# One tile and one transfer per MB of weights, a transfer limit in the planner, and split first transposes

## The chip, the cores and the metric

The kernel runs on one core of one Trainium2 chip. Its time is device microseconds of that core, from launch to end; a profile's span runs from the core's first to its last instruction. Engines are named as in the profile: PE (TensorE, matmul), PEld (its weight loads), DVE (VectorE), ACT (ScalarE), POOL (GpSimd) and SP (SyncE, which here issues nearly all DMAs).

## What is computed

x is 2048 rows of 1024 (bf16). Two layers, each of two steps with the same weights:

```python
x = x + A(layernorm(x), wqkv, wo)
x = x + B(layernorm(x), w1, b1, w2, b2)
...
def A(x, wqkv, wo):          # 32 heads of 32; a window of 8 keys, every second row back
    q, k, v = split(x @ wqkv)
    logits = q . k[pos - 2 * w] / sqrt(32), w = 0..7, masked where pos - 2 * w < 0
    return (softmax(logits) . v) @ wo
def B(x, w1, b1, w2, b2):    # 1024 -> 3584 -> 1024
    return relu(x @ w1 + b1) ** 2 @ w2 + b2
```

## The kernel before, in words

**Units.** Even and odd rows are held apart, so that the window's stride of two becomes one. The 2048 rows of a layer are cut into four blocks of 512; a block of a layer is a unit, u = 0 to 7. A unit goes through SA (load x, layer norm, transpose to `xnA`), the projections to q, k and v (`SQ` plain, `SQ7` with seven products), S2 (attention, mostly DVE), SW or SW7 (projection with wo, layer norm into `xnB`), SF1 (w1, squared relu, into `r2`) and SF2 (w2). `build` interleaves them: while unit u is in SW and SF1, unit u + 1 is in its projections and attention.

**Seven products.** From unit 1 on (SF1), and from unit 2 on (q, k, v), a matrix product of 2 x 2 blocks is made of seven products in place of eight. A step has seven of them, numbered 1 to 7. Products 1, 2 and 4 use raw blocks of the weights; 5, 6, 7 and 3 use combinations (sums and differences of raw blocks), which DVE forms once while the first units run (`keep_wqkv`, `keep_w1`) and which are stored to scratch in DRAM (`wqs`, `w1s`) as 128 x 1024 f16 cells of 256 KB. On the moving side stand the activations `xnA` or `xnB` and their combinations `TA` or `T`. A product is eight matmuls of 256 columns (`product`, L658). `interleave` sets the order: product pr of step i sorts by 7 i + AT[pr], so neighbouring steps overlap. SF1 has seven steps (49 products), the job "k" two (14), the job "qv" four (28).

**Loads of the weights.** `seven` (L564) walks this order in groups of four products. A group has one tile `w` of 128 x 4 x 4 x 256 (1 MB): its raw blocks first, each by a transfer of its own of 256 KB (rows of 2 KB out of the weight matrix), then its combinations, one transfer of 256, 512 or 768 KB from that group's scratch. `cells` says which place in which tile a product has. A product waits for its own place alone.

**The planner.** Nothing is issued as it is written: `Plan.add` collects operations with engine, estimated duration, priority and the cells that they read and write. `Plan.schedule` runs them through a list scheduler with classes of buffers: twelve of 8 KB per partition, of which at most eight for weight tiles `w` (`caps`); the others hold `xnA`, `xnB`, `T`, `TA`, attention products and so on. A DMA is charged `mb / DMA_MBS` on one common line plus a latency. `emit` makes the order that each engine's instructions then have, in order, on the chip; `ORDER` is a list of seeds by which priorities are shifted slightly ahead of each pass. The planner knew no limit to the number of transfers under way. On the chip, SP's transfers use eight semaphores in turn, and SP waits where the one whose turn it is still belongs to a transfer that hasn't landed.

**The start.** In unit 0 the first tiles of x are normalised by DVE (`ln_first`), transposed by PE into PSUM (`transpose`, L802, eight blocks of 128 x 128) and copied by one DVE instruction of 1024 columns into `xnA` (L805). `SQ(0, "kq")` runs its first sixteen chunks for the first half of the rows alone (`halves`); a chunk is eight matmuls (L877) over the eight blocks. Weights of unit 0 come in pieces of 512 KB.

Names of the profile: `in_B_w_dram` at L658 is w1, `in_A_wqkv_dram` wqkv, `w1s`, `wqk` and `wqqv` are scratch of combinations; L402 is the helper `dma`, L768 the transposing DMA.

Of the kernel before, what the change touches and what calls it, by code (L numbers as in the profile page):

```python
# [52 lines left out]
RAW = {1: (0, 0), 2: (0, 1), 4: (1, 1)}  # L53
PR1 = 20.0
# [19 lines left out]
DMA_MBS = 0.38  # L74
OWN_LAT = {"DVE": 0.12, "ACT": 0.1}
# [4 lines left out]
def act(n):  # L80
    return 0.05 + n * 0.00084

# [34 lines left out]
class Plan:  # L117
# [45 lines left out]
    def schedule(self):  # L163
# [46 lines left out]
        dma_free = 0.0  # L210
        out = []
        t = 0.0
        left = len(self.ops)
        while left:
            progress = False
            for e in engs:
# [28 lines left out]
            while True:  # L245
                if own is None:
                    offer((o.prio, next(seq), o))
                elif o is not None:
# [9 lines left out]
                    if not own:  # L258
                        for b in o.bufs:
# [55 lines left out]
class _Kernel:  # L315
# [19 lines left out]
    def setup(self):  # L335
# [36 lines left out]
        self.order1 = self.interleave(range(self.NDP))  # L372
        self.orderq = {"k": self.interleave([("k", 0), ("k", 1)]), "qv": self.interleave([("q", 0), ("q", 1), ("v", 0), ("v", 1)])}
        self.wqs = {j: self.scratch(tc, o, f"wq{j}") for j, o in self.orderq.items()}
        self.two = [tc.dram_tile([128, 2, 4, BLK], F16, name=f"two{i}") for i in range(2)]
        self.w1s = self.scratch(tc, self.order1, "w1s")

# [32 lines left out]
    def wqkv_block(self, nm, ms, n=1):  # L410
        i = 4 * "qkv".index(nm) + ms
        return self.wqkv[i * 128:(i + n) * 128]

    def wqkv_raw(self, d, m, k):
        nm, s = d
        return self.wqkv_block(nm, 2 * m + s)[:, k * 1024:(k + 1) * 1024]

    def w1_raw(self, dp, m, k):
        return self.w1[dp * 128:(dp + 1) * 128, m * 2048 + k * 1024:m * 2048 + (k + 1) * 1024]
# [5 lines left out]
    def cells(self, order):  # L425

        at = {}
        for j in range(0, len(order), 4):
            part = order[j:j + 4]
            raw = [d for d in part if d[1] in RAW]  # L430
            for i, d in enumerate(raw + [d for d in part if d[1] not in RAW]):
                at[d] = j // 4, i, len(raw)
        return at

    def scratch(self, tc, order, name):

        n = [0] * (-(-len(order) // 4))
        for (d, pr), (t, i, r) in self.cells(order).items():
            n[t] += pr not in RAW
        return [tc.dram_tile([128, max(c, 1), 4, 256], F16, name=f"{name}{t}") for t, c in enumerate(n)]  # L440
# [71 lines left out]
    def interleave(self, todo):  # L512

        return [(d, pr) for _, d, pr in sorted((7 * i + AT[pr], d, pr) for i, d in enumerate(todo) for pr in AT)]

    def keep_wqkv(self, nm, ws, after=()):
# [3 lines left out]
        at = self.cells(self.orderq[job])  # L520

        def one(s):
# [5 lines left out]
            def comb(t, a, b, op, r, pr):  # L528
                p.add("DVE", dve(1024), lambda: nc.vector.tensor_tensor(t[:], a(), b(), op), r, [(t, 0)], self.nxt(), after, name="tq")
                j, i, n = at[(nm, s), pr]  # L530
                self.dma(lambda: self.wqs[job][j][:, i - n], lambda: t[:], [(t, 0)], [(("wqs", job, j), i)], 0.26, prio=50.0, name="wqst", lat=4.0)
# [8 lines left out]
    def SQ7(self, u, job):  # L540
# [8 lines left out]
        self.seven(self.orderq[job], self.wqs[job], ("wqs", job), self.wqkv_raw, st["xnA"], st["TA"], lambda d: self.qkv_step(u, *d))  # L549
# [14 lines left out]
    def seven(self, order, store, key, raw, xnT, T, make):  # L564

        rhs = self.rhs_blocks(xnT, T)
        at = self.cells(order)
        self.ffs = []
        steps, ws = {}, {}
        for d, pr in order:  # L570
# [12 lines left out]
            if d not in steps:  # L583
                steps[d] = make(d)
            steps[d](pr, ws[t], i, *rhs[pr])
# [7 lines left out]
    def qkv_step(self, u, nm, s):  # L593
# [29 lines left out]
        def mul(pr, w, wi, rhs, rc):  # L623
            bank, fm = self.product(pr, w, wi, rhs, X, Y, Z)
            self.state[u]["gate" + nm] = p.add("PE", 8 * MMH, fm, rc + [(w, wi)], [(bank, 0)], self.nxt(), name="fq")
# [36 lines left out]
    def keep_w1(self, dp, w):  # L662

        nc, p = self.nc, self.p
        at = self.cells(self.order1)
# [4 lines left out]
        def store(pr, src, r):  # L670
            j, i, n = at[dp, pr]
            self.dma(lambda: self.w1s[j][:, i - n], src, r, [(("w1s", j), i)], 0.26, prio=50.0, name="w1st", lat=4.0)
# [41 lines left out]
    def ln(self, x, xv, xcells, xnT, tl, prio, vec, on_pe=False, tag="xn", after=(), vnorm=True):  # L714
# [25 lines left out]
        else:  # L740
# [18 lines left out]
            if vnorm:  # L759
                p.add("DVE", 0.45, f3v, xr + [(sm, 1)], [(xn, 0)], -99.5, name="ln3")  # L760
            else:
                p.add("ACT", 1.15, f3, xr + [(sm, 1)], [(xn, 0)], prio - 0.2, name="ln3")
        if on_pe:
            self.transpose(xn, xnT, tl, -10.0)
            return
# [5 lines left out]
    def ln_first(self, x, xv, xnT, tl, after=()):  # L771
# [19 lines left out]
        def rest(after=()):  # L791
            p.add("DVE", 0.5, f4, [(x, 0), (sm, 0), (sm, 1)], [(xn, 0)], -2e5 + pr, after=after, name="bn4")
            return self.transpose(xn, xnT, tl, -1e5 + pr, act=tl in CP), xn
        return bn, ag, rs, rest

    def transpose(self, xn, xnT, tl, prio, act=False):
        nc, p, KD = self.nc, self.p, self.KD
        pt = Buf("ps", "pt", [128, KD, 128], F16, "partial")

        def f5():  # L800
            for kd in range(KD):
                nc.tensor.transpose(pt[:, kd, :], xn[:, kd * 128:(kd + 1) * 128], self.ident[:])  # L802

        def f6():
            (nc.scalar.copy if act else nc.vector.tensor_copy)(xnT[:, tl], pt[:])  # L805
        p.add("PE", 0.65, f5, [(xn, 0)], [(pt, 0)], prio, name="pt")
        return p.add("ACT" if act else "DVE", 1.05 if act else 0.69, f6, [(pt, 0)], [(xnT, tl)], prio - 200.0, name="ptc")
# [11 lines left out]
    def SA(self, u):  # L819
        layer, b = divmod(u, self.NB)  # L820
# [26 lines left out]
    def SQ(self, u, jobs, order=None, halves=()):  # L847
# [10 lines left out]
        for ms in range(4) if u == 0 else (0, 2):  # L858
            for nm in jobs:
                w = ws[nm][ms // 2]  # L860
                if u == 0:
# [8 lines left out]
        def chunk(nm, c0, hs):  # L870
# [4 lines left out]
            def fm():  # L875
                for kd in range(KD):
                    nc.tensor.matmul(pq[:, t0 * HB:t1 * HB], w[:, c0 // 2 % 2, kd // 4, kd % 4, c0 % 2 * 128:c0 % 2 * 128 + 128],  # L877
                                     xnT[:, 2 * t0:2 * t1, kd, :], start=(kd == 0), stop=(kd == KD - 1))
            st["gate" + nm] = self.pe(4 * len(hs), fm, [(xnT, i) for i in range(2 * t0, 2 * t1)] + [(w, c0 // 2 % 2)], [(pq, h) for h in hs], name="pq")
# [3 lines left out]
        for nm, c0 in halves:  # L883
            chunk(nm, c0, (0,))
# [307 lines left out]
    def SF1_plain(self, u):  # L1192
# [8 lines left out]
        def load(dp):  # L1201
            w = Buf("8K", "w", [128, 2, 8, 256], BF)
            for m in range(2):
                self.dma(lambda m=m: w[:, m].rearrange("p k n -> p (k n)"), lambda m=m: self.w1[dp * 128:(dp + 1) * 128, m * 2048:(m + 1) * 2048],
# [38 lines left out]
        for i, (dp, pr) in enumerate(self.interleave(range(PLAIN1, self.NDP))):  # L1243
# [12 lines left out]
    def SF1(self, u):  # L1256
# [8 lines left out]
        self.seven(self.order1, self.w1s, ("w1s",), self.w1_raw, xnT, T, lambda d: self.ffn1_step(r2, d, u in FOLD))  # L1265
        st["gatef"] = self.ffs[40]

    def ffn1_step(self, r2, dp, fold):
# [51 lines left out]
        def mul(pr, w, wi, rhs, rc):  # L1320
            bank, fm = self.product(pr, w, wi, rhs, X, Y, Z)
            self.ffs.append(p.add("PE", 8 * MMH, fm, rc + [(w, wi[0] if isinstance(wi, tuple) else wi or 0)], [(bank, 0)], self.nxt(), name="ff"))
# [218 lines left out]
def _lay(name, a):  # L1541

    if name == "A_wqkv":
# [32 lines left out]
```

## Time and profile before

| | before |
|---|---|
| median of 3 runs, us | 1143.18 (1141.79 to 1144.17) |
| profiled execution, us | 1140.7 |
| its span, us | 1139.0 |
| mean granted clock of PE | 0.998 |
| DMA packets | 176799, 362.37 MB |
| HBM read, written | 314.84 MB, 31.46 MB |

How to read it: a row of a group gives busy time, the mean of one instruction in ns, and the idle time just ahead of it with what ended it. A wait row reads "engine line of who waited <- engine, tile and line of what it waited for: total us, times, longest". SPq is SP's queue, that is, its issuing of DMAs. In a row of stretches stand, after the stretch and its length, each engine's busy us with its number of instructions, the granted clock, the DMA engines' share, and GB/s. A matmul's busy time includes its passage through the array, so neighbours overlap; a product of eight matmuls advances PE by less than its busy time. The DMA share of a stretch can be over 100%.

### The profile page before, as it was taken

How to read it: one execution, taken by the hardware profiler on the slowest of the kernel's cores; microseconds unless marked ns; L12 is line 12 of the kernel's file. 1: busy time of each engine (PE TensorE's matmuls, PEld its weight loads, DVE VectorE, ACT ScalarE, POOL GpSimd, SP SyncE). 2: the span in 40 equal slices, each digit the busy share in tenths (PEclk: the TensorE clock that was granted, in tenths of full speed). 3: DMA queues.
4: the chain of work that ended last, by engine and by line, in shares of the span. 5: the costliest groups of instructions: out<-in, count | busy, mean ns of one | idle time of the engine just before them, and what ended most of it. 6: DMA issues, size and time to landing. Idle time of an engine off the chain costs nothing.

```text
span 1139.0 us, 20967 instructions
## 1 busy us (share of the span) xinstructions
PE 1124.7 (99%) x7873; PEld 772.6 (68%) x7919; DVE 998.5 (88%) x1539; ACT 802.2 (70%) x1602; POOL 1.8 (0%) x8
## 2 busy tenths in 40 slices
PE   8999999998999999999999999999999999999998
PEld 6645764677846787468864688657885678845864
DVE  7999999998699998979999699996999889996341
ACT  6734997567984789757994679847798477943861
POOL 0000000000000000000000000000000000000000
PEclk9999999999999999999999999999999999999999
DMA  9967679999999998999979997899989999699982
GB/s 366 290 212 255 223 265 312 326 357 332 399 322 360 331 368 299 333 383 301 397 256 349 403 306 304 314 313 393 318 330 325 377 349 352 256 343 279 368 281 80
DMA packets 176799, 362.37 MB, mean 318 GB/s; under 512 B 71866, under 2 KB 80186, under 8 KB 174778
## 3 DMA queue, kind: packets, MB, share of 16 engines
q1 hardware_dynamic: 176410, 360.51, 93.2%
q8 instruction: 62, 1.02, 0.4%
q10 hardware_dynamic: 288, 0.52, 0.1%
q14 instruction: 39, 0.32, 0.1%
HBM read 314.84 MB, written 31.46 MB: 304 GB/s over the span
## 4 chain that ended last, share of the span: by engine, by line
PE 89%; DVE 4%; ACT 3%; DMA 3%; issue 1%; SPq 0%; DVEq 0%; ACTq 0%
PE X L658 24%; PE X L1375 14%; PE Z L658 12%; PE pq L877 7%; PE Z L1375 7%; PE Y L658 6%; PE py L478 4%; PE py L1071 4%; PE Y L1375 3%; PE X L1142 3%; PE lg L952 2%; PE Z L1142 1%; DMA w<-in_B_w_dram 1%; ACT r L1310 1%; PE Y L1142 1%
## 5 line engine op out<-in xcount | busy, mean ns | idle before, releaser
L658 PEld LDWEIGHTS <-w 128*128 128x128 bf16 (+1 forms) x4904 | 480.0, 98 | 75.6 <-DMA w<-in_B_w_dram 3.6
L1375 PEld LDWEIGHTS <-r 128*128 128x128 f16 x1183 | 115.7, 98 | 135.9 <-issue 1.7
L1375 PE MATMUL X<-w,r 128*128 128x512 f16 (+2 forms) x784 | 176.5, 377 | 1.1 <-ACT yxa L1044 0.5
L937 DVE TENSOR_TENSOR P<-q,k 128x2048 f16<-128x2048 f16 x128 | 154.0, 1224 | 5.0 <-PE lg L952 4.4
L658 PE MATMUL X<-T,w 128*128 128x256 f16 x1224 | 154.7, 274 | 3.3 <-DMA w<-in_B_w_dram 3.3
L1016 DVE TENSOR_TENSOR pr<-pb,v 128x4096 f16<-128x4096 f16 x64 | 146.3, 2296 | 1.1 <-PE X L658 0.7
L945 DVE TENSOR_TENSOR P<-P,P 128x2048 f16<-128x2048 f16 x106 | 129.3, 1221 | 0.3
L1310 ACT ACTIVATE r<-rr 128x1024 f16<-128x1024 f16 x110 | 124.6, 1143 | 1.3 <-DVE rr L1306 1.1
L1023 DVE TENSOR_TENSOR pr<-pr 128x2048 f16<-128x2048 f16 (+1 forms) x128 | 118.4, 953 | 0.1
L658 PE MATMUL X<-TA,w 128*128 128x256 f16 x864 | 108.5, 273 | 0.0
L591 ACT COPY Y<-X 128x512 f32<-128x512 f32 x115 | 69.9, 608 | 27.1 <-PE X L658 22.9
L877 PE MATMUL pq<-xnA,w 128*128 128x256 f16 (+1 forms) x512 | 86.6, 326 | 0.4 <-DMA w<-in_A_wqkv_dram 0.4
L1293 DVE TENSOR_TENSOR rr<-u,y 128x512 f16<-128x512 f16 x110 | 46.3, 423 | 33.2 <-ACT y L1289 17.2
L1289 ACT CAST y<-Z 128x512 f16<-128x512 f32 x110 | 69.3, 647 | 5.3 <-PE Z L658 4.0
L877 PEld LDWEIGHTS <-w 128*128 128x128 bf16 x512 | 49.8, 98 | 33.0 <-DMA w<-in_A_wqkv_dram 0.7
L1316 ACT ACTIVATE rr<-X,b1T 128x256 f16<-128x256 f32 x110 | 55.0, 558 | 5.3 <-PE X L658 5.1
L1316 ACT ACTIVATE rr<-Y,b1T 128x256 f16<-128x256 f32 x110 | 53.3, 531 | 4.3 <-PE Y L658 3.8
L658 PE MATMUL Y<-xnB,w 128*128 128x256 f16 x440 | 56.0, 273 | 0.1
L658 PE MATMUL X<-xnB,w 128*128 128x256 f16 x440 | 55.7, 273 | 0.0
L609 ACT CAST u<-X 128x512 f16<-128x512 f32 x72 | 41.8, 586 | 18.9 <-PE X L658 18.9
L613 ACT CAST yq<-Z 128x512 f16<-128x512 f32 x72 | 41.7, 587 | 18.3 <-PE Z L658 16.5
L658 PE MATMUL Z<-T,w 128*128 128x256 f16 x392 | 50.6, 273 | 0.6 <-DVE halo L913 0.5
(159 smaller groups left out, 1649.9 us busy)
## 6 DMA issues: line engine op xcount, KB each, us to landing
w<-tw SPq DMA_DIRECT2D x56, 896.0 KB, 6.1
w<-in_B_w_dram SPq DMA_DIRECT2D x147, 256.0 KB, 7.5
w<-in_B_w_dram SPq DMA_DIRECT2D x42, 896.0 KB, 7.6
w<-w1s SPq DMA_DIRECT2D x56, 512.0 KB, 7.9
w<-in_A_wqkv_dram SPq DMA_DIRECT2D x108, 256.0 KB, 6.2
w<-w1s SPq DMA_DIRECT2D x28, 768.0 KB, 8.1
w<-wqqv SPq DMA_DIRECT2D x30, 512.0 KB, 6.2
w<-in_B_w_dram SPq DMA_DIRECT2D x28, 512.0 KB, 6.1
```

Source lines behind the costliest of these rows:

```text
L591: self.p.add("ACT", act(512), lambda: self.nc.scalar.copy(Y[:], X[:]), [(X, 0)], [(Y, 0)], UP, name="u")
L658: nc.tensor.matmul(bank[:, a, :], lw[:, k, a * 128:(a + 1) * 128], rhs(k), start=(start and k == 0 and a == 0), stop=(k == 3), skip_group_ ...
L877: nc.tensor.matmul(pq[:, t0 * HB:t1 * HB], w[:, c0 // 2 % 2, kd // 4, kd % 4, c0 % 2 * 128:c0 % 2 * 128 + 128], xnT[:, 2 * t0:2 * t1, kd, ...
L937: nc.vector.tensor_tensor(cur[:], q[:, c, None, hb * HB:(hb + 1) * HB].to_broadcast([128, W, HB]), _win_ap(k[:, c, :], HALO + hb * HB, HB) ...
L945: nc.vector.tensor_tensor(other[:], other[:], cur[:], ALU.add)
L1016: p.add("DVE", dve(4096), lambda pr=pr, ch=ch: nc.vector.tensor_tensor(pr[:], pb[:].unsqueeze(1).to_broadcast([128, 2, W, HB]), _win_ap2(v ...
L1023: nc.vector.tensor_tensor(dst, pr[:, :, 0:n, :], pr[:, :, n:2 * n, :], ALU.add)
L1142: nc.tensor.matmul(bank[q][:], left(j, q), right(j), start=start and j == 0, stop=j == h - 1, skip_group_check=True)
L1289: p.add("ACT", act(512), lambda: nc.scalar.copy(y[:], bank[:]), [(bank, 0)], [(y, 0)], 1.5, name="y")
L1310: p.add("ACT", 0.955, lambda: nc.scalar.activation(out=r2[:, f:f + 2, :].rearrange("p a t -> p (a t)"), in_=r[:].rearrange("p a m t -> p ( ...
L1316: p.add("ACT", 0.36, lambda a=a: nc.scalar.activation(out=r[:, a, 0, :], in_=bank[:, a, :], func=ACTF.Relu, bias=self.b1T[:, f + a:f + a + ...
L1375: nc.tensor.matmul(banks[q][:, lo:hi], left(jj, q), w[:, j, lo:hi], start=(start and jj == 0), stop=(jj == h - 1), skip_group_check=True)
```

## The change

1. **Raw tiles.** All raw blocks are laid out once more in the order of use behind the weight matrix (a rearrangement of the input array), four to a tile: `raw_tiles`. One contiguous transfer of 1 MB with 8 KB rows (256, 512 KB where fewer are left) loads four.
2. **Combination tiles.** The four combinations of a step have one scratch tensor and one tile, loaded by one transfer of 1 MB. `cells` and its places go.
3. **Waits.** A product waits for its whole tile (cell `(w, 0)`).
4. **The planner** refuses a DMA while the seventh-last is still under way in its model (`LANES = 7`), looks at every engine again when a DMA ends, and has new seeds (`ORDER`: 48, 29 and 30 in place of 47, 26 and 18).
5. **First transposes.** For the first two tiles of unit 0, transposes and copies go by halves (four blocks, 512 columns); the first chunk of `SQ(0, "kq")` is two operations of four matmuls, the first of which needs the first halves only.
6. v of unit 0 is loaded in two transfers of 1 MB in place of four of 512 KB.

```diff
+COMB = (5, 7, 6, 3)
+RT = 4
+LANES = 7
...
         def fits(o):
+            if o.mb and len(landed) >= LANES and landed[-LANES] > t + 1e-9:
+                return False
...
                     end = dma_free
+                    landed.append(end + o.lat)
...
                     if not own:
+                        if o.mb:
+                            fresh.update(engs)
...
+    def raw_tiles(self, ap, at, n):
+        tiles = []
+        for i in range(0, n, RT):
+            k = min(RT, n - i) * 1024
+            tiles.append(ap[at:at + 128 * k].rearrange("(p n) -> p n", n=k))
+            at += 128 * k
+        return tiles
...
+    def scratch(self, tc, todo, name):
+        return {d: tc.dram_tile([128, 4, 4, 256], F16, name=f"{name}{i}") for i, d in enumerate(todo)}
...
         for d, pr in order:
-            t, i, nr = at[d, pr]
-            if t not in ws:
-                w = ws[t] = Buf("8K", "w", [128, 4, 4, 256], F16)
-                mine = [(j, e) for e, (s, j, _) in at.items() if s == t]
-                for j, (e, q) in mine:
-                    if q in RAW:
-                        self.dma(lambda w=w, j=j: w[:, j].rearrange("p k n -> p (k n)"), lambda e=e, q=q: raw(e, *RAW[q]), (), [(w, j)], 0.256,
-                                 name="w", cast=BF)
-                cs = [j for j, (e, q) in mine if q not in RAW]
-                if cs:
-                    self.dma(lambda w=w, a=nr, b=nr + len(cs): w[:, a:b], lambda t=t: store[t][:], [(key + (t,), j) for j in cs],
-                             [(w, j) for j in cs], len(cs) * 0.256, name="w")
+            if pr in RAW:
+                if nr % RT == 0:
+                    w = ws["raw"] = Buf("8K", "w", [128, 4, 4, 256], F16)
+                    n = min(RT, 3 * len(self.scr[job]) - nr)
+                    self.dma(lambda w=w, n=n: w[:, 0:n].rearrange("p i k n -> p (i k n)"), lambda t=nr // RT: raws[t], (), [(w, 0)], n * 0.256,
+                             name="w", cast=BF)
+                w, i = ws["raw"], nr % RT
+                nr += 1
+            else:
+                if d not in ws:
+                    w = ws[d] = Buf("8K", "w", [128, 4, 4, 256], F16)
+                    key = (job,) + (d if isinstance(d, tuple) else (d,))
+                    self.dma(lambda w=w: w[:], lambda d=d: self.scr[job][d][:], [(key, i) for i in range(4)], [(w, 0)], 4 * 0.256, name="w")
+                w, i = ws[d], COMB.index(pr)
...
-        p.add("PE", 0.65, f5, [(xn, 0)], [(pt, 0)], prio, name="pt")
-        return p.add("ACT" if act else "DVE", 1.05 if act else 0.69, f6, [(pt, 0)], [(xnT, tl)], prio - 200.0, name="ptc")
+            p.add("PE", 0.65 / parts, f5, [(xn, 0)], [(pt, i)], prio, name="pt")
+            op = p.add("DVE", 0.09 + 0.6 / parts, f6, [(pt, i)], [(xnT, tl if i == parts - 1 else (tl, i))], prio - 200.0, name="ptc")
+        return op
...
+            for i in range(parts):
+                xc = [(xnT, t if i == parts - 1 else (t, i)) for t in range(2 * t0, 2 * t1)]
+                st["gate" + nm] = self.pe(4 * len(hs) / parts, lambda i=i: fm(i), xc + [(w, c0 // 2 % 2)], [(pq, h) for h in hs], name="pq")
...
         for nm, c0 in halves:
-            chunk(nm, c0, (0,))
+            chunk(nm, c0, (0,), 2 if (nm, c0) == halves[0] else 1)
```

More of the change, by code (lines that the diff above doesn't have):

```diff
@@ L81, in act, with interleave @@
     return 0.05 + n * 0.00084
+def interleave(todo):
+    return [(d, pr) for _, d, pr in sorted((7 * i + AT[pr], d, pr) for i, d in enumerate(todo) for pr in AT)]
 def mix(x):
@@ L210, in schedule @@
         dma_free = 0.0
+        landed = []
         out = []
@@ L371, in setup @@
         self.NDP = KF // 4
-        self.order1 = self.interleave(range(self.NDP))
-        self.orderq = {"k": self.interleave([("k", 0), ("k", 1)]), "qv": self.interleave([("q", 0), ("q", 1), ("v", 0), ("v", 1)])}
-        self.wqs = {j: self.scratch(tc, o, f"wq{j}") for j, o in self.orderq.items()}
+        todo = {"k": [("k", 0), ("k", 1)], "qv": [("q", 0), ("q", 1), ("v", 0), ("v", 1)], "w1": list(range(self.NDP))}
+        self.orders = {j: interleave(d) for j, d in todo.items()}
+        self.scr = {j: self.scratch(tc, d, f"s{j}") for j, d in todo.items()}
+        self.raws = {"k": self.raw_tiles(self.wqkv, 3 * D * D, 6), "qv": self.raw_tiles(self.wqkv, 3 * D * D + 6 * 128 * 1024, 12),
+                     "w1": self.raw_tiles(self.w1, D * self.F, 3 * self.NDP)}
         self.two = [tc.dram_tile([128, 2, 4, BLK], F16, name=f"two{i}") for i in range(2)]
-        self.w1s = self.scratch(tc, self.order1, "w1s")
         p = self.p
@@ L423, in w2_block @@
         return self.w2[i * 128:(i + 1) * 128]
[L425 to L440, printed above, removed]
+    def scratch(self, tc, todo, name):
+        return {d: tc.dram_tile([128, 4, 4, 256], F16, name=f"{name}{i}") for i, d in enumerate(todo)}
     def keep_w2(self, j0, n, w):
@@ L548, in SQ7 @@
             st["TA"] = self.rhs_combos(st["xnA"], 1.0, "8K", "TA", True)
-        self.seven(self.orderq[job], self.wqs[job], ("wqs", job), self.wqkv_raw, st["xnA"], st["TA"], lambda d: self.qkv_step(u, *d))
+        self.seven(job, st["xnA"], st["TA"], lambda d: self.qkv_step(u, *d))
         for nm in job:
@@ L759, in ln @@
             if vnorm:
-                p.add("DVE", 0.45, f3v, xr + [(sm, 1)], [(xn, 0)], -99.5, name="ln3")
+                p.add("DVE", 0.45, f3v, xr + [(sm, 1)], [(xn, 0)], pv, name="ln3")
             else:
@@ L763, in ln @@
         if on_pe:
-            self.transpose(xn, xnT, tl, -10.0)
-            return
+            return self.transpose(xn, xnT, tl, -10.0 if pv == -99.5 else pv, parts), xn
         def f5():
@@ L857, in SQ @@
             ws[nm] = [Buf("8K", "w", [128, 2, 2, 4, 256], BF) for _ in range(2)]
-        for ms in range(4) if u == 0 else (0, 2):
+        pieces = u == 0 and len(jobs) > 1
+        for ms in range(4) if pieces else (0, 2):
             for nm in jobs:
                 w = ws[nm][ms // 2]
-                if u == 0:
+                if pieces:
                     self.dma(lambda w=w, ms=ms: w[:, ms % 2].rearrange("p a k n -> p (a k n)"), lambda nm=nm, ms=ms: self.wqkv_block(nm, ms), (),
@@ L868, in SQ, with chunk @@
             order = [(nm, c0) for nm in jobs for c0 in range(NCH)]
-        def chunk(nm, c0, hs):
+        def chunk(nm, c0, hs, parts=1):
             pq = Buf("ps", "pq", [128, BLK], F32)
@@ L1242, in SF1_plain @@
         self.ffs, steps = st["phs"], {}
-        for i, (dp, pr) in enumerate(self.interleave(range(PLAIN1, self.NDP))):
+        for i, (dp, pr) in enumerate(interleave(range(PLAIN1, self.NDP))):
             if dp not in steps:
@@ L1264, in SF1 @@
         T = self.rhs_combos(xnT, -60.0, "8K", "T")
-        self.seven(self.order1, self.w1s, ("w1s",), self.w1_raw, xnT, T, lambda d: self.ffn1_step(r2, d, u in FOLD))
+        self.seven("w1", xnT, T, lambda d: self.ffn1_step(r2, d, u in FOLD))
         st["gatef"] = self.ffs[40]
@@ L1321, in mul @@
             bank, fm = self.product(pr, w, wi, rhs, X, Y, Z)
-            self.ffs.append(p.add("PE", 8 * MMH, fm, rc + [(w, wi[0] if isinstance(wi, tuple) else wi or 0)], [(bank, 0)], self.nxt(), name="ff"))
+            self.ffs.append(p.add("PE", 8 * MMH, fm, rc + [(w, wi[0] if isinstance(wi, tuple) else 0)], [(bank, 0)], self.nxt(), name="ff"))
             if pr == 1:
@@ L1541, in _lay, with raws @@
 def _lay(name, a):
+    import numpy as np
+    def raws(blocks, todo):
+        seq = [blocks(d, *RAW[pr]) for d, pr in interleave(todo) if pr in RAW]
+        return [np.stack(seq[i:i + RT], 1).reshape(-1) for i in range(0, len(seq), RT)]
     if name == "A_wqkv":
-        a = a.reshape(2, 4, 128, 3, 128, 4, 2).transpose(3, 5, 2, 0, 1, 6, 4).reshape(1536, 2048)
+        a = a.reshape(2, 4, 128, 3, 128, 4, 2).transpose(3, 5, 2, 0, 1, 6, 4).reshape(3, 4, 128, 2, 1024)
+        get = lambda d, m, k: a["qkv".index(d[0]), 2 * m + d[1], :, k]
+        a = np.concatenate([a.reshape(-1)] + raws(get, [("k", 0), ("k", 1)]) + raws(get, [("q", 0), ("q", 1), ("v", 0), ("v", 1)]))
     elif name == "A_wo":
```

58 lines of the change are left out of this document (27 added, 31 removed), and 16 rows, old and new, of the table ORDER.

## The prediction

> **What bounds the kernel now.** First the page: busy time of each engine and the DMA queue's share.
>
> ```profile
> span 1139.0 us, 20967 instructions
> PE 1124.7 (99%) x7873; PEld 772.6 (68%) x7919; DVE 998.5 (88%) x1539; ACT 802.2 (70%) x1602; POOL 1.8 (0%) x8
> ...
> q1 hardware_dynamic: 176410, 360.51, 93.2%
> ```
>
> PE is busy for 1124.7 of 1139.0 us, so all its idle time together is 14.3 us. The change alters no product, so no more than that can come back, and part of it lies before the first and after the last matmul. SP's queue holds the 16 DMA engines for 93% of the span: two resources are nearly full. Next, what PE waited for, longest first:
>
> ```profile
> PE X L658 <- DMA w<-in_B_w_dram: 3.3, 1, 3.3
> PE pt L802 <- DVE xn L784: 1.8, 1, 1.8
> ...
> PE X L1375 <- ACT yxa L1044: 0.5, 1, 0.5
> PE Z L658 <- DVE halo L913: 0.5, 1, 0.5
> ```
>
> One wait in the middle is worth looking at: 3.3 us for a raw block of w1. The other long one (1.8 us) is the first layer norm. Around the 3.3 us, the stretches (PE, PEld, DVE, ACT and POOL busy, granted clock, DMA share, GB/s):
>
> ```profile
> 260.00:271.50 11.50, 11.50 (x106) 10.09 (x104) 11.50 (x22) 8.86 (x17) 0.00 (x0) 1.00 1.05 316
> 271.50:274.90 3.40, 0.06 (x2) 0.03 (x2) 3.40 (x6) 0.83 (x2) 0.00 (x0) 0.92 1.01 375
> 274.90:278.40 3.50, 3.50 (x18) 2.31 (x19) 2.20 (x2) 1.60 (x4) 0.00 (x0) 0.59 1.00 351
> 278.40:312.00 33.60, 33.60 (x304) 29.54 (x303) 22.18 (x37) 33.51 (x71) 0.00 (x0) 1.00 1.01 391
> ```
>
> PE stands still for 3.34 us (3.40 less 0.06), and in the 3.5 us behind it the granted clock is 0.59, which costs 3.5 x 0.41 = 1.4 us more. The stop is worth 4.8 us. It falls in SF1 of unit 1. The chain of waits says how it came about:
>
> ```profile
> 255.81 0.87 PE Y L658 x8
> ...
> 257.50 7.28 DMA w<-w1s
> 264.78 0.02 issue
> 264.80 10.03 DMA w<-in_B_w_dram
> ```
>
> The late load was issued 0.02 us after another load had landed and took 10.03 us itself: SP was held by a transfer in flight, not by a buffer. Over the span, SP's own waits:
>
> ```profile
> SPq L402 <- PE X L658: 91.6, 49, 10.9
> SPq L402 <- PE Z L658: 64.6, 18, 10.9
> SPq L402 <- DMA w<-w1s: 57.5, 54, 3.2
> ...
> SPq L402 <- DMA w<-in_B_w_dram: 31.6, 78, 2.3
> ```
>
> It waits longest for PE to give buffers back (156.2 us in two rows), which is harmless, as such loads are ahead of their use; and 89.1 us in two rows, 132 times, for transfers in flight.
>
> **Part 1, fewer and larger loads.** The loads of the seven-product jobs:
>
> ```profile
> w<-in_B_w_dram SPq DMA_DIRECT2D x147, 256.0 KB, 7.5
> ...
> w<-w1s SPq DMA_DIRECT2D x56, 512.0 KB, 7.9
> w<-in_A_wqkv_dram SPq DMA_DIRECT2D x108, 256.0 KB, 6.2
> w<-w1s SPq DMA_DIRECT2D x28, 768.0 KB, 8.1
> ...
> w<-in_A_wqkv_dram SPq DMA_DIRECT2D x6, 1024.0 KB, 9.2
> ```
>
> Before: 147 + 84 for w1, 108 raw ones for q, k, v, and by the code 6 x 4 and 6 x 7 from scratch, 405 in all. After: SF1 takes 6 raw and 7 combined tiles in each of 7 units (91), k 2 + 2 and qv 3 + 4 in each of 6 (66), 157 in all. Bytes are the same; 248 issues leave SP. A 1024 KB load lands in 9.2 us, a 256 KB one in 6.2 to 7.5, so seven in flight hold four times a raw block's bytes. What the engines gain I take from two 4 us stretches, 137.5 to 141.5 us with 2 KB rows nearly alone and 494 to 498 us with 8 KB rows:
>
> ```profile
> DMA packets 864, 1.61 MB, mean 401 GB/s; under 512 B 80, under 2 KB 80, under 8 KB 864
> q1 hardware_dynamic: 864, 1.61, 105.3%
> ```
>
> ```profile
> DMA packets 224, 1.70 MB, mean 426 GB/s; under 512 B 16, under 2 KB 16, under 8 KB 16
> q1 hardware_dynamic: 224, 1.70, 101.6%
> ```
>
> Divided by their shares these are 1.61/4/1.053 = 0.382 and 1.70/4/1.016 = 0.418 MB per us. The 255 raw blocks are 66.8 MB: 174.9 us of the queue's time now, 159.8 after, so 15 us fewer, from 93.2% to about 92% of the span. All of it lies beside PE. It is worth time only where a load is late, which is the one place above; the 10 or so raw blocks just ahead of it (2.6 MB) save 6.9 - 6.3 = 0.6 us there.
>
> **Part 2, what the larger tile costs.** (a) A product now waits for its whole tile, and product 1 of a job needs a raw and a combined tile, 2.1 MB where 1.05 MB did. Counting the interleaved order through, the bytes needed by a given product are equal or 1.05 MB more, never 2; at the tenth product of SF1, where the stop is, they are equal. (b) A tile is held longer: its four products lay next to each other, 4 x 0.87 = 3.5 us; now they spread over 7 to 9 places, up to 7.9 us. SF1 uses 13 tiles in 49 x 0.87 = 42.6 us, one in 3.3. With eight tiles allowed, issue to last use is 8 x 3.3 = 26 us, so 22.7 us to the first use before and 18.3 after; less 8.1 and 9.2 to land, a margin of about 14.6 shrinks to 9. That costs nothing in a steady stretch: SP's long waits for PE are the cover. It begins to cost when only five tiles can be had (16.5 - 7.9 - 9.2 is below zero), because the twelve 8 KB buffers are shared with activations and attention. (c) Stores into scratch stay 256 KB each and as many: nothing. (d) v of unit 0 in two 1 MB loads in place of four: its first use comes long after, nothing.
>
> **Part 3, the planner.** It now refuses a transfer while seven are under way, so SP's order fits what SP really does; and its seeds give another order on every engine. PE's work is the same, so the effect is only in stops. No row prices a new order. Bounds: it takes away the 4.8 us and both stops of 0.5 (-5.8), or leaves them and adds as much (+5.8). I take the long stop gone, because its last link is exactly what the planner now knows and the load behind it is now in one of a third as many transfers; and I add 1.0 us of new short stops, as many as the two rows of 0.5, since an order never fits everywhere.
>
> **Part 4, the first transposes by halves.**
>
> ```profile
> 8.68 1.43 DVE L805 COPY xnA<-pt 128x1024 f16<-128x1024 f16 x2
> ...
> 10.16 1.03 PE L877 MATMUL pq<-xnA,w 128*128 128x256 f16 x8
> 11.61 0.61 PE L877 MATMUL pq<-xnA,w 128*128 128x256 f16 x4 [0.41 <-DMA w<-in_A_wqkv_dram]
> ```
>
> The two copies end at 10.11 and PE starts 0.05 later. In halves, each between 0.36 (half) and 0.71 us (the same), PE's first half can start up to 0.36 earlier. But the next chunk waits for its weights until 11.61, which the change doesn't move, so the gain lies between 0 and 0.7 (0.36 and the wait filled by another chunk). I take 0.3. The two extra copies cost DVE between nothing and 1.4 us; PE's wait for weights until 11.61 covers that, and without it the 1.4 would eat the gain.
>
> **The sum.** -4.8 + 1.0 - 0.3 = -4.1 us. The profiled execution took 1140.7 us (span 1139.0 and 1.7 around it): 1136.6 for one like it. The median of the runs is 2.5 above it, so 1143.2 - 4.1 = **1139.1 us**.
>
> **Rivals.** *The stop stays.* DMA is at 1.05 in 260 to 271.5 and moves only 316 GB/s, against 391 at 1.01 later, so the load may be late for bytes, not for its place in line; freeing SP then changes nothing. For it: the share. Against: 0.6 us less work ahead, another order. Time: 1143.2 - 0.3 = 1142.9.
>
> *Slower: the first tiles of SF1 in unit 1.* The place has no margin:
>
> ```profile
> 252.08 0.33 SPq L402 DMA_DIRECT2D w<-w1s  x1
> ...
> 260.01 1.04 PE L658 MATMUL X<-xnB,w 128*128 128x256 f16 x8
> ```
>
> ```profile
> w<-w1s SPq DMA_DIRECT2D x1, 512.0 KB, 7.9
> ```
>
> The first combined part lands at 260.0, PE starts the job at 260.01. Another 1.05 MB wanted by product 1, at 316 GB/s, is 3.3 us of stop on top of the present one: 1143.2 + 3.3 - 0.3 = 1146.2. It decides as soon as SP's order doesn't bring that load at least 3.3 us sooner. Against it: products of qv still interleave there and can fill.
>
> *Slower: small transfers behind large ones.* DVE already waits for the transposed activations of SF1:
>
> ```profile
> DVE T L695 <- DMA xnB<-xn: 5.7, 4, 2.4
> ```
>
> In four places that DMA is late now and PE hides it. With two more 1.05 MB loads ahead, at the 391 GB/s of 278 to 312 us, it comes 5.4 us later; where PE has nothing else left, that stop and its slow clock cost 6.8. Two such places less the gain of 5.1: 1143.2 + 8.5 = 1151.7. It decides if loads are queued deep, which the waits for PE's buffers speak against. The Trainium skill, "DMA: Bandwidth & Descriptors", section "Queues, rings and completion order", says that each engine consumes descriptors in ring order, so that a short transfer doesn't pass a long one on SP's row; the late load above, which needed 10.03 us for 256 KB, agrees. By that rule the time would be the 1151.7 of this rival, if the queue is deep.
>
> **How the numbers follow.** Forecast 0.57; stop stays 0.16; first tiles 0.17; small transfers 0.10. Faster by over 0.2% (2.3 us, about what a measurement tells from no change) is the first, 0.57; within it the second, 0.16; slower the last two, 0.27. Low end: every stop of the trace gone (-4.8 - 1.0 - 0.3 = -6.1), in an execution as quick as the profiled one, 1140.7 - 6.1 = 1134.6. High end 1148: past the first-tile rival by 1.8, which leaves out the last. For the forecast alone the range is 1134.6 to 1141.
>
> **What would show it.** Right: no wait of PE over 1 us for a `w` load after the start, granted clock 1.00 from 260 to 300 us, SP's waits on transfers far below 89 us, PE busy still 1124 us or a little less. Wrong: a PE wait on `raw` or scratch tiles at the beginning of a job with a clock under 1 behind it (first tiles); DVE's wait on xnB well over 5.7 us (small transfers); the same 3.3 us at another time (bytes). A new stop on DVE or ACT in PE's list would mean that the order, not the loads, made the difference.

## The result and the profile after

| | before | after |
|---|---|---|
| median, us | 1142.32 (6 runs, 1139.83 to 1144.17) | 1134.36 (6 runs, 1132.48 to 1135.21) |
| profiled execution, us | 1140.7 | 1134.86 |
| its span, us | 1139.0 | 1133.1 |

The ratio of the times is 0.9931, 95% interval 0.9915 to 0.9948: faster by 0.7%, 8.0 us, where 4.1 were forecast. The time lies 4.7 us under the forecast and just under the low end of its range. The prediction starts from 1143.18, the median of three of the six runs before; that of all six is 1142.32.

The page of the changed kernel, busy time and DMA queue (packets, MB, share of 16 engines' span):

```profile
span 1133.1 us, 20734 instructions
PE 1122.6 (99%) x7872; PEld 771.8 (68%) x7919; DVE 996.4 (88%) x1541; ACT 800.2 (71%) x1602; POOL 1.8 (0%) x8
...
q1 hardware_dynamic: 140666, 360.50, 91.3%
```

PE's idle time fell from 14.3 to 10.5 us, its busy time by 2.1: matmuls at a slow clock are counted as busy, and the prediction's 1.4 us of slow clock were among them (the row from 274.90 has PE busy throughout). Where the other 0.7 come from isn't shown. The queue's share fell from 93.2% to 91.3% at the same bytes. What PE waited for (sum in us, times, longest):

```profile
PE pt L800 <- DVE xn L781: 1.9, 1, 1.9
...
PE X L657 <- DMA w<-in_B_w_dram: 0.8, 2, 0.5
PE py L479 <- ACT py L492: 0.5, 1, 0.5
```

The 3.3 us for a block of w1 have become two waits of at most 0.5. The stretches around that place:

```profile
260.00:271.50 11.50, 11.14 (x102) 9.51 (x99) 10.89 (x19) 7.85 (x16) 0.00 (x0) 1.00 1.00 359
271.50:274.90 3.40, 2.94 (x28) 2.41 (x26) 3.16 (x7) 2.54 (x5) 0.00 (x0) 1.00 1.06 299
274.90:278.40 3.50, 3.50 (x32) 2.85 (x30) 3.43 (x3) 3.25 (x8) 0.00 (x0) 1.00 1.00 414
```

The clock stays at 1.00; DMA is as full as before and moves 359 GB/s where it moved 316. SP's waits:

```profile
SPq L416 <- PE X L657: 196.6, 78, 8.3
...
SPq L416 <- DMA w<-in_A_wqkv_dram: 18.0, 14, 2.2
...
SPq L416 <- DMA w<-in_B_w_dram: 7.4, 7, 2.1
```

For buffers that PE holds it now waits 196.6 us in the first row (91.6 before). Over all rows of this view that name a DMA, the sum is 67.6 us in 59 waits, before 171.2 us in 256. SP is ahead of PE far more than it was. The start:

```profile
9.96 2.78 PE L879 MATMUL pq<-xnA,w 128*128 128x256 f16 x24
12.59 0.61 PE L800 MATMUL pt<-ident,xn 128*128 128x128 f16 x8
```

The first chunk starts 0.2 us sooner, and 24 matmuls follow one another with no wait for weights. Before, the transposes now at 12.59 started at 13.37. The transposes that open the work, before and then after, start at slightly different times too:

```profile
8.02 1.35 PE L802 MATMUL pt<-ident,xn 128*128 128x128 f16 x16 [1.76 <-DVE xn L784]
...
13.37 0.61 PE L802 MATMUL pt<-ident,xn 128*128 128x128 f16 x8
```

```profile
7.91 1.36 PE L800 MATMUL pt<-ident,xn 128*128 128x128 f16 x16 [1.88 <-DVE xn L781]
```

So the start is 0.8 us shorter, not 0.3. Of this, 0.1 is the first layer norm, which ended sooner in this execution; from the first transposes on it is 5.35 us before and 4.68 after, 0.7 less.

### The profile page after: what moved, and what is told of

Read it like the earlier page. It is cut to its first block, busy times and chain, and to the rows that moved or that the text cites. A ratio compares the mean times of both kernels' runs of the same rounds, so it can differ in the third digit from the quotient of the medians.

```text
span 1133.1 us, 20734 instructions
## 1 busy us (share of the span) xinstructions
PE 1122.6 (99%) x7872; PEld 771.8 (68%) x7919; DVE 996.4 (88%) x1541; ACT 800.2 (71%) x1602; POOL 1.8 (0%) x8
## 3 DMA queue, kind: packets, MB, share of 16 engines
q1 hardware_dynamic: 140666, 360.50, 91.3%
## 4 chain that ended last, share of the span: by engine, by line
PE 90%; ACT 5%; DMA 3%; issue 1%; DVE 0%; DVEq 0%; SPq 0%; ACTq 0%
PE X L657 25%; PE X L1379 14%; PE Z L657 12%; PE Z L1379 7%; PE pq L879 7%; PE Y L657 6%; PE py L1075 4%; PE Y L1379 3%; PE py L479 3%; PE X L1146 3%; PE lg L956 1%; PE Z L1146 1%; ACT r L1314 1%; DMA w<-in_B_w_dram 1%; ACT u L1287 1%; ACT rr L1320 1%
## 5 line engine op out<-in xcount | busy, mean ns | idle before, releaser
L657 PEld LDWEIGHTS <-w 128*128 128x128 f16 (+1 forms) x4904 | 479.5, 98 | 72.2 <-DMA w<-in_B_w_dram 1.3
L1027 DVE TENSOR_TENSOR pr<-pr 128x1024 f16<-128x1024 f16 (+1 forms) x128 | 118.4, 955 | 0.0
L657 PE MATMUL X<-xnB,w 128*128 128x256 f16 x440 | 55.9, 273 | 0.8 <-DMA w<-in_B_w_dram 0.8
L657 PE MATMUL Z<-xnB,w 128*128 128x256 f16 x392 | 50.8, 273 | 0.1
## 6 DMA issues: line engine op xcount, KB each, us to landing
w<-sqv SPq DMA_DIRECT2D x24, 1024.0 KB, 11.2
```

What stands on the lines that cost most here:

```text
L657: nc.tensor.matmul(bank[:, a, :], lw[:, k, a * 128:(a + 1) * 128], rhs(k), start=(start and k == 0 and a == 0), stop=(k == 3), skip_group_ ...
L1027: nc.vector.tensor_tensor(dst, pr[:, :, 0:n, :], pr[:, :, n:2 * n, :], ALU.add)
```

## The experiments

All kernels that start from the changed one keep its planned order on every engine, except where the seeds or the limit are taken away. Edits are shown in short form. The last column is SP's waits for transfers in flight, the sum over all rows of that view that name a DMA, in the profiled execution.

| kernel | median, us | ratio to before, 95% interval | SP's waits for DMA, us (times) |
|---|---|---|---|
| before, again (e1) | 1144.32 | 0.9999, 0.998 to 1.0017 | 180.7 (263) |
| changed, again (e2) | 1134.82 | 0.9924, 0.99 to 0.9948 | 67.1 (60) |
| all loads split (e3) | 1143.1 | 0.9993, 0.9975 to 1.0012 | 198.2 (282) |
| whole first transposes (e4) | 1134.76 | 0.9924, 0.9901 to 0.9947 | 64.8 (59) |
| raw tiles in 4 x 256 KB, 2 KB rows (e5) | 1138.64 | 0.9958, 0.9939 to 0.9978 | 184.7 (211) |
| combined tiles in 2 x 512 KB (e6) | 1136.29 | 0.9938, 0.9915 to 0.996 | 130.4 (134) |
| raw tiles in 4 by partitions, 8 KB rows (e7) | 1239.02 | 1.0832, 1.0789 to 1.0875 | 346.5 (281) |
| raw tiles in one transfer, 2 KB rows (e8) | 1136.61 | 0.9945, 0.9924 to 0.9965 | 55.9 (56) |
| 216 small transfers added (e9) | 1141.1 | 0.9977, 0.9963 to 0.999 | 208.4 (154) |
| before, raw blocks merged (e10) | 1136.56 | 0.9947, 0.9932 to 0.9963 | 115.9 (143) |
| changed, no seeds (e11) | 1159.39 | 1.014, 1.0124 to 1.0156 | 44.0 (48) |
| before, no seeds (e12) | 1156.12 | 1.012, 1.0096 to 1.0143 | 208.3 (303) |
| empty instructions on SP (e13) | 1134.83 | 0.9919, 0.9901 to 0.9937 | 59.3 (57) |
| changed, no seeds, no limit (e14) | 1154.51 | 1.0096, 1.0077 to 1.0115 | 48.8 (53) |

**e1, the kernel before once more.**

> The kernel before, unchanged, to see other executions of it. Theory A (the gain over the forecast is the one long stop of PE in SF1 of unit 1, which is longer in most executions than in the profiled one): this profile shows the stop at 265 to 280 us again, 3 to 8 us long with the slow clock behind it, and runs with a longer span have a mean granted clock of 0.997 to 0.998. Rival B (the stop of the first profile was an accident, and before loses its time in many short waits): the stop is absent or under 1 us here, and other waits make up the span of 1138 to 1142 us.

This execution has a span of 1143.0 us. PE's waits in it:

```profile
PE X L658 <- DMA w<-in_B_w_dram: 3.1, 1, 3.1
PE Z L658 <- ACT yq L613: 1.7, 1, 1.7
...
PE Z L658 <- DVE T L695: 1.6, 1, 1.6
...
PE Z L658 <- DVE TA L699: 0.8, 1, 0.8
```

The long stop is there again, hardly other in size (3.1 for 3.3 us). What makes this execution 4 us longer are three waits that the first profile doesn't have, 4.1 us together. They name ACT and DVE. Behind T (1.6 us) stands a transposing DMA, for which DVE waited 2.3 us; ahead of TA (0.8 us) DVE was at work without a pause, so no transfer shows there. The chain of waits shows the one on ACT (1.7 us) to be a late transfer too:

```profile
766.19 9.35 DMA out_dram<-xo
...
775.61 0.59 ACT yq L613
```

A store of 128 KB took 9.35 us (7.77 in the first profile), and ACT could not go on until it had landed. So half of theory A fell (the stop isn't longer) and rival B holds in part: the rest is short waits, 3.3 of the 4.1 us behind late small transfers.

**e2, the changed kernel once more.**

> The changed kernel, unchanged, on the same chip as the three others. Both theories: ratio to the kernel before 0.991 to 0.995, mean granted clock 0.999 to 1.000, and waits of PE for w around 260 and 272 us of 0.3 to 0.8 us each.

As expected in the ratio, not in the waits: the two for `w` around 260 and 272 us aren't there, and PE waits 1.1 us for wo and 0.5 us for TA instead.

**e3, the loads of before in the new order.**

```diff
-self.dma(w[:, 0:n], raws[t], ..., n * 0.256, cast=BF)
+for j, (e, q) in enumerate(seq[nr:nr + n]): dma_start(w[:, j], raw_of(job, e, *RAW[q]))
-self.dma(w[:], self.scr[job][d][:], ..., 4 * 0.256)
+for a in (0, 2): dma_start(w[:, a:a + 2], self.scr[job][d][:, a:a + 2])
```

> The changed kernel with its order on every engine, its tiles and its planner, but each raw tile is loaded by transfers of 256 KB out of the weight matrix (2 KB rows, as before) and each combined tile by two of 512 KB. Theory A1 (the size and number of the transfers made the gain): SP waits for transfers again, the stop in SF1 of unit 1 comes back with 2 us or more, time 3 to 6 us above the changed kernel (ratio to before 0.996 to 0.999). Rival A2 (the new order made it): within 1.5 us of the changed kernel (ratio 0.992 to 0.995), although SP's waits for transfers rise from about 50 to over 100 us.

The whole gain is gone: 8.3 us above the changed kernel measured beside it, more than the 3 to 6 that A1 expected. A2 falls: the order without the loads is worth nothing against before. (The order was planned for the large loads, so this doesn't say what the best order for the small ones would give.) But the loss doesn't sit where A1 put it: the stop in SF1 of unit 1 is 1.3 us here. PE's largest waits, and the chain ahead of the worst of them:

```profile
PE Z L668 <- DVE T L704: 3.7, 3, 2.1
...
PE X L668 <- DMA w<-sw: 1.3, 1, 1.3
```

```profile
532.22 10.45 DMA xnB<-xn
...
543.60 1.35 PE Z L668 x8
```

T was late, and PE with it, three times. The transpose of `xnB` took 10.45 us, but the same one took 10.55 in e2. What differs is when SP came to it; its issue in e2, then in e3:

```profile
525.66 3.49 SPq L765 DMA_TRANSPOSE xnB<-xn  x1
```

```profile
532.22 5.31 SPq L776 DMA_TRANSPOSE xnB<-xn  x1
```

It was issued 6.6 us later, where PE was only 3.6 us behind, and the 2.15 us of the stop follow. In e1 PE waits for T as well.

**e4, first transposes whole.**

```diff
-for kd in range(i * n, (i + 1) * n):
+for kd in range(KD) if i == 0 else ():
...
-nc.vector.tensor_copy(xnT[:, tl, i * n:(i + 1) * n], pt[:, i * n:(i + 1) * n])
+if i == 0: nc.vector.tensor_copy(xnT[:, tl], pt[:])
```

> The changed kernel and its order, but the first two transposes and their copies are made whole, at the place of their first halves. If the halves are worth what the prediction took: 0.3 us more than the changed kernel, not to be told in the times (ratio to before 0.992 to 0.995), and PE's first chunk starts at about 10.2 us in place of 9.96 us. Rival (the start is worth more, as the second chunk no longer waits for weights): 0.7 us or more, with PE idle between 10 and 13 us.

The first chunk of projections in this kernel's timeline of PE (start, length, instruction, tiles and shapes):

```profile
10.20 2.78 PE L880 MATMUL pq<-xnA,w 128*128 128x256 f16 x24
```

The chunk starts 0.24 us later (10.20 against 9.96), but the first transposes do so by 0.15:

```profile
8.06 1.35 PE L800 MATMUL pt<-ident,xn 128*128 128x128 f16 x16 [2.04 <-DVE xn L781]
```

From the first transposes to the chunk it is 2.14 us whole and 2.05 in halves, so the halves are worth about 0.1 us, which the time can't tell. The chunks follow without a gap here too, and the weights land no sooner than before (the fourth load of them at 11.4 us, before at 11.6), so the other 0.6 us at the start come from the order, which lets another chunk fill the wait for weights.

**e5, e6, e8: the loads one by one.**

```diff
e5, e6: one of the two edits of e3 alone
e8: -tiles.append(ap[at:at + 128 * k].rearrange("(p n) -> p n", n=k))
    +tiles.append(ap[at:at + 128 * k].rearrange("(i p n) -> p i n", p=128, n=1024))
```

> The changed kernel and its order; only the raw tiles are loaded as before, four transfers of 256 KB with 2 KB rows each; combined tiles stay one transfer. Theory A (number of transfers: SP, which issues in order, must wait for one of its transfers in flight to land): most of the loss of the kernel with all loads split (8.3 us) is here, as 98 transfers are added for each 33 of the combined ones, 4 to 8 us above the changed kernel, with SP's waits for transfers over 80 us. Theory B (row size: 2 KB rows keep the DMA engines busy longer): the same. A2 (combined tiles matter more): under 3 us.

> The changed kernel and its order; only the combined tiles are loaded by two transfers of 512 KB, with 4 KB rows. A: 73 more transfers, 1 to 3 us above the changed kernel. B: rows of 4 KB are moved nearly as fast as rows of 8 KB, under 1 us.

> The changed kernel and its order; each raw tile is still one transfer of 1 MB, but its blocks lie one behind the other in DRAM, so that its rows are 2 KB. A (number of transfers): within 1.5 us of the changed kernel. B (row size): 4 to 8 us above it, with the DMA queue's share up by 1 to 2 points.

The changed kernel wasn't measured beside these; against its median in e2 (1134.82), e5 loses 3.8 us, e6 1.5, e8 1.8. The last two lie well within the intervals, and that of e5 (0.9939 to 0.9978) overlaps e2's (0.99 to 0.9948) at its end. Rows of 2 KB in one transfer leave SP's waits as they are (55.9 us) and raise the queue's share from 91.3% to 92.6%:

```profile
q1 hardware_dynamic: 164090, 360.50, 92.6%
```

That is hardly clear of the changed kernel itself, which had 90.9% to 92.1% in other executions. B's 4 to 8 us are not there. Four transfers of the same rows bring SP's waits to 184.7 us, but 3.8 us are just short of A's 4 to 8. By the code the edits add 183 transfers (e5) and 85 (e6), where the expectations counted fewer, so an added transfer comes to about 0.02 us in both. Together, in e3, the two splits cost more (8.3) than one by one (5.3).

**e7, as many transfers with 8 KB rows.**

```diff
+for j in range(0, 128, 128 // n): dma_start(w[j:j + 128 // n, 0:n], raws[t][j:j + 128 // n])
```

> The changed kernel and its order; each raw tile is loaded by four transfers (by quarters of the partitions), each with 8 KB rows: as many transfers as with the loads of before, but the packets of the changed kernel. A (number of transfers): as slow as the four transfers with 2 KB rows, 4 to 8 us above the changed kernel. B (row size): within 1.5 us of the changed kernel, although SP's waits for transfers are over 80 us.

It was meant to part number from row size and didn't: 104 us slower. DMA packets and the load queue on its page:

```profile
DMA packets 143983, 362.37 MB, mean 294 GB/s; under 512 B 70794, under 2 KB 79114, under 8 KB 123530
...
q1 hardware_dynamic: 143594, 360.51, 97.6%
```

The transfers into 32 partitions are slow in themselves: there are as many packets of 8 KB as in the changed kernel, but the median one takes 353 ns in place of 309 and the mean is 459 in place of 324. Neither theory had that, and why it is so stays open.

**e9, more transfers, no more bytes.**

```diff
+for _ in range(3):   # behind each raw tile's load
+    i = self.tiny = (self.tiny + 1) % 16
+    nc.sync.dma_start(self.spare[0:16, i * 16:i * 16 + 16], self.x_par[0, 0:16, i * 16:i * 16 + 16])
```

> The changed kernel, its order, its tiles and its loads, and behind each of the 72 raw tiles' loads three more transfers of 512 bytes each (16 partitions x 32 bytes) into a spare tile that nothing reads: as many transfers as with raw blocks of 256 KB, hardly any more bytes. A (number of transfers): SP waits for transfers as long as with four raw blocks per tile (over 100 us) and the time goes up by 2 us or more. B (size of the rows and bytes): within 1 us of the changed kernel (ratio to before 0.992 to 0.994).

6.3 us slower than the changed kernel (e2), at 0.1 MB more and a queue's share of 92.3%. B falls, and both numbers of A come true. SP's waits:

```profile
SPq L420 <- DMA w<-in_B_w_dram: 55.4, 27, 2.9
SPq L420 <- DMA w<-sw: 29.3, 20, 3.0
...
SPq L420 <- DMA w<-two: 17.1, 8, 2.7
```

L420 is the line that issues the small transfers: SP waits there for the large ones ahead of it to land, and whatever it would issue next waits with it. The small transfers themselves take nearly as long to land as the loads of 256 KB that are left (7.3 us):

```profile
spare<-in_A_x_dram SPq DMA_DIRECT2D x216, 0.5 KB, 7.2
```

PE has the same order as in e2, so its matmuls can be compared one by one. Most of the loss arises in one stretch: a matmul that e2 has at 250.5 us comes 1.1 us later here, one at 283.7 us 4.9 later, and the end 6.3 later. It is the stretch of the long stop of before.

**e10, the old order with fewer transfers.**

```diff
-for j, (e, q) in mine:   # one transfer for each raw block of the tile
-    if q in RAW: self.dma(w[:, j], raw(e, *RAW[q]), ...)
+    if not done: done.append(1); dma_start(w[:, 0:nr], self.packed[job, t])
```

> The kernel before with its order, tiles and planner; where a tile has two raw blocks, they come in one transfer of 512 KB (4 KB rows, from a second layout of the weights), 98 transfers fewer in all. If the transfers alone make the gain, whatever the order: 2 to 5 us faster than before (ratio 0.9955 to 0.998), the stop in SF1 of unit 1 under 2 us and its clock at 1.0. If the order and the planner's limit are needed too: within 1.5 us of before, stop as long as it was.

0.9947 is better than the best that was expected. With its own order, its tiles and a planner that knows of no limit, the kernel before gains 6.8 us, where the change gains 8. (The merged loads have rows of 4 KB in place of 2, so here number and row size change together; e8 and e9 part them, in the changed kernel.) What PE still waited for after its start:

```profile
PE X L1389 <- ACT yxa L1058: 1.3, 1, 1.3
...
PE Z L672 <- DVE TA L713: 0.4, 1, 0.4
PE X L1389 <- ACT X L500: 0.2, 1, 0.2
```

No load of weights is among it: the stop in SF1 of unit 1 is gone without a new order.

**e11, e12, e14: without seeds.**

```diff
-ORDER = [...]
+ORDER = []
e14 besides: -LANES = 7
             +LANES = 10000
```

> The changed kernel without the seeds: the planner runs once, with the priorities as written. If the gain is in loads and planner: within 4 us of the changed kernel and faster than before (ratio under 0.998). If the seeds carry it: slower than before, 1145 us or more.

> The kernel before without its seeds, the pair to the changed kernel without seeds. If loads and planner make the gain: both lose about as much by it, and the difference between the pair stays 5 to 10 us. If the seeds carry it: the pair is within 3 us.

> The changed kernel without seeds and without the planner's limit of seven transfers. If the limit is worth anything by itself: slower than the changed kernel without seeds (1159.4 us) by 2 us or more. If it isn't: within 2 us of it, or faster.

Without seeds both kernels are slower than before, the changed one by 25 us and the other by 13, and the pair is 3.3 us apart, the changed one behind; within 3 was expected if the seeds carry it. The difference of 5 to 10 isn't there: in these two plans the loads gain nothing. In the changed one without seeds (e11) it is ACT that PE waits for most, by PE's waits:

```profile
PE Y L1370 <- ACT Y L581: 7.1, 5, 1.7
PE X L1370 <- ACT r L1305: 4.9, 4, 2.7
```

SP's waits for transfers are only 44.0 us, and over all rows PE waits 16.7 us for ACT and 2.8 us for loads. In e12 PE waits 15.2 us for ACT. That may be why the large loads save nothing in this pair; it isn't shown. Without the planner's limit (e14) the changed one is 4.9 us faster than with it (1.0096 against 1.014, intervals apart, though measured at different times). By itself the limit is worth nothing here; this is one pair of plans, and what it is worth together with seeds wasn't tried.

**e13, SP held without a transfer.**

```diff
+for _ in range(24): nc.sync.nop(nofuse=True)   # behind each raw tile's load
```

> The changed kernel, its order and its loads; behind each of the 72 raw tiles' loads SP executes 24 empty instructions in place of the three small transfers, so that its queue is held for some time but no transfer is added. Theory A (the eight transfers in flight are the limit): within 1.5 us of the changed kernel (ratio 0.992 to 0.994), SP's waits for transfers about 67 us as without. Rival A' (SP's own time per issued transfer is what costs): slower by 3 to 6 us like the small transfers, if the pause is about 1 us.

The empty instructions aren't in the trace; in the timeline of SP the next transfer is issued 0.05 us after a raw tile's, at once:

```profile
401.40 0.33 SPq L416 DMA_DIRECT2D w<-in_B_w_dram  x1
401.78 0.42 SPq L416 DMA_DIRECT2D w<-sw  x1
```

So it is the changed kernel a third time and doesn't decide between A and A'. It stays open which share of e9's loss is SP's waiting for transfers (141 us more than in e2) and which its own time for issuing 216 more of about 0.35 us (some 75 us).

## Why the prediction was right in direction and half in size

- **The long stop** (-4.8): right. 3.3 us of waiting and the slow clock behind it are gone, and e10 shows that fewer and larger raw loads alone do it.
- **The step that failed** is in the sum: "The median of the runs is 2.5 above it", carried over as if every kernel had it. The stops that the sum prices are those of one execution, and a quick one; a usual one of the kernel before loses time that this trace doesn't show. e1, an execution of 1144.75 us, has 4.1 us more of waits, 3.3 of them behind late small transfers. Nor is the offset a constant: the changed kernel's median lies 0.5 us below its profiled execution here, 0.9 above in e2 and 1.8 above in e13. It was luck which execution was profiled. The 2.5 that was added and the 0.5 that came make 3.0 of the 4.7 us; 0.9 of the 2.5 were the small number of runs. That the waits of e1 are those of a usual execution is not shown beyond this one trace. The low end of the range has the same fault: it took the stops of one trace for all there were.
- **New short stops** (+1.0): not there on balance. There are waits of about 0.5 us in the new profile, but as many of the old ones went. With the start, 0.8 in place of 0.3, this is 1.5 of the other 1.7 us.
- **"It is worth time only where a load is late, which is the one place above"** (part 1): wrong as to the one place. The place is the most sensitive one (e9 loses 3.8 of its 6.3 us there without a byte to speak of), but e1 and e3 lose microseconds in others, where a transpose or a store comes late, and the prediction gave these no term. Larger rows were to save the DMA engines 15 us. Between e8 and the changed kernel it is 15 us (92.6% of 1133.3 against 91.3% of 1133.1), though executions of one kernel differ as much; in time it is worth at most the 1.8 us of e8.
- **The planner** (part 3) got the credit for the stop, and e10 takes it away: the old planner's order is nearly as good once it has fewer transfers. That the new order as such makes the gain falls with e3. The seeds are another matter: 13 us (e12) and 25 us (e11) hang on them, more than on the change. How far the 8 us depend on the luck of two sets of seeds isn't shown.
- **Larger tiles held longer** (part 2): no cost was seen. SP waits more for PE's buffers, and in its profile no load makes PE wait over 0.5 us, though the tiles of 1 MB took 8.7 to 11.2 us to land (medians of their groups) where 9.2 was taken.
- **First transposes** (part 4): 0.3 was taken, and 0.7 came: about 0.1 from the halves (e4) and 0.6 from another chunk that fills the wait for weights, which the prediction had as its upper bound.
- **The rivals.** First tiles: two waits of at most 0.5 us at 260 and 272 us are what is left of it. The prediction had product 1 wait for a raw and a combined tile; by the code it uses a raw block alone, so 1.05 MB in place of 0.26, and both tiles must have landed before product 5, the next one, can start. Small transfers behind large ones: the rule of order that it used is borne out, as in the profiles before and after no transfer lands ahead of one that SP issued earlier (743 and 524 landings that the traces tell). The transposes of `xnB` do land later after their issue (median 7.8 us, 6.4 before). But DVE's wait for them, in the changed kernel's waits of DVE, fell, and one wait for `xnA` came, behind which PE has no wait in this profile:

```profile
DVE TA L697 <- DMA xnA<-xn: 4.4, 1, 4.4
...
DVE T L693 <- DMA xnB<-xn: 0.2, 1, 0.2
```

  So late small transfers do cost time, and the prediction put them on the wrong side: with many transfers in the row SP comes to them late, as e3 shows against e2, and this outweighs the longer way to landing behind large ones.

## What to carry to other kernels

Count transfers as well as bytes: where one queue issues in order and waits for its transfers in flight, each additional transfer can hold up the next urgent one, even one of 512 bytes (e9). Look at that queue's waits for DMAs against its waits for the consumer's buffers; when the first are large, merge loads before touching the order. And when the profiled execution is quicker than the median, ask what the others have more of before carrying the difference over: it may be just what the change removes.

## What the runs showed of the hardware

A transfer of 512 bytes held its place in the row like one of 256 KB (e9: 7.2 us to land in the median, and 6.3 us of time for 216 of them; e5: 3.8 us for four in place of one for each raw tile). A load of 256 KB into 32 partitions landed later than the same bytes into 128 (medians of 9.3 and 11.8 us in e7, 6.8 and 8.4 in e5, for the blocks of wqkv and of w1). And PE's clock: a stop of 1.7 us left it alone, one of 2.2 us was followed by a slow clock, but one of 3.5 us in e7 was not. So from these traces the length of a stop alone doesn't decide. In the stretches of e1, then of e3, then of e7, the clock is the third number from the end:

```profile
774.40:776.20 1.80, 0.12 (x2) 0.00 (x0) 0.00 (x0) 0.59 (x2) 0.00 (x0) 1.00 1.03 427
776.20:779.60 3.40, 3.35 (x31) 3.00 (x31) 0.85 (x2) 2.68 (x5) 0.00 (x0) 1.00 1.01 400
```

```profile
541.40:543.80 2.40, 0.25 (x3) 0.22 (x3) 1.11 (x4) 0.59 (x1) 0.00 (x0) 1.00 1.01 328
543.80:547.60 3.80, 3.80 (x22) 2.69 (x21) 3.80 (x6) 1.43 (x3) 0.00 (x0) 0.55 1.04 402
```

```profile
261.60:265.10 3.50, 0.00 (x0) 0.00 (x0) 2.48 (x7) 0.57 (x1) 0.00 (x0) 1.00 1.07 389
265.10:268.00 2.90, 2.79 (x24) 2.27 (x24) 2.90 (x4) 1.17 (x2) 0.00 (x0) 1.00 1.10 226
```

So the stops of 3.3 us (before, quoted in the prediction) and 2.2 us (e3) cost 1.4 and 1.7 us (3.8 x 0.45) on top of what they last, and those of 1.7 us (e1) and 3.5 us (e7) nothing.
